# A limit on outstanding bytes beside a limit on outstanding transfers

## The chip, the cores and the metric

The kernel runs on one core of a Trainium2 chip. The metric is the time of one execution on the device in microseconds (us), the median of the runs shown. The engines are TensorE (PE, with its weight loads PEld), VectorE (DVE), ScalarE (ACT), GpSimd (POOL) and SyncE (SP). Here SP does nothing but issue transfers between the chip's main memory and the on-chip buffers; ACT issues four of them, at the start.

## The reference

The inputs are q, k and v of 8 batches, 8 heads, 576 positions and 64 values. Two attentions are added, one over means of 4 neighbouring positions, one over a band of 7 positions. Their sum goes through a gated layer:

```python
q_d = q.reshape(B, H, Sd, factor, D).mean(axis=3)      # k_d, v_d likewise, factor 4
out_up = np.repeat(sm_attn(q_d, k_d, v_d), factor, axis=2)
mask = np.abs(pos[:, None] - pos[None, :]) < factor
out_local = softmax(where(mask, scale * q @ k.T, -1e9)) @ v
x = (out_up + out_local).transpose(0, 2, 1, 3).reshape(B, S, H * D)
h = gelu(x @ w_in)                                      # 512 -> 1024
u, v = h[..., :512], h[..., 512:]
v_n = (v - mean(v)) / sqrt(var(v) + 1e-6) * g_ln
gated = u * (einsum('ts,bsd->btd', w_sg, v_n) + b_sg[None, :, None])
out = x + gated @ w_out
```

w_in, w_sg, b_sg, g_ln and w_out are the same for all batches. w_in and w_out arrive as 64-bit numbers.

## The kernel before

The work is cut into some 2,100 small tasks with names. A long string, ORDER, gives their order by hand; each task's instructions are appended to the queues of its engines in that order, and every engine works its own queue off in order. Attention runs per pair of heads: 32 groups, 4 for each batch. After a batch's four groups its gated layer runs, and its PE work is laced between the attention groups of the next batches.

Names of a group's tasks (a number behind the letters is the group):

- `lq`, `lk`, `lv`, `lw` load q, k, the values for the pooled attention (v) and for the band (vw). q and k are 293 KB, vw 320 KB; v is two transfers of 224 KB, for the first four groups four of 96 KB.
- `S` is the band's scores on PE, `Y` the pooled scores (from group 4 on both together, `YS`). `mx`, `nx` are maxima and biases, `ea`, `eb`, `ec` the exponentials on ACT, `np`, `nq` the divisions. `T`, `U`, `t` transpose on PE, `pa` to `pe` copy the results out, `D` multiplies by the values (L604 for the pooled ones, L620 for the band's). `xa` to `xl` make the sum x and split it into a high and a low half.

In the gated layer `v` is the second half of x @ w_in (L722), `u` the first half, `s` the product with w_sg, `o` the product with w_out (all three are L800), and `os` stores 288 KB of the result.

The weights are loaded as 64-bit words, 512 KB at a time: `wy0` to `wy3` (the v half of w_in), `wz0` to `wz3` (the u half), `wr0` to `wr3` (w_out). Each goes through a chain of small tasks: `wu` (ACT, L346) and `wq` (ACT L334, or DVE L336) work on the two words, `wb` on DVE (L340, L342) shifts, `wt` (POOL, L350) adds, `wh` and `wl` make a high and a low half. `wq0` to `wq4` without a letter load w_sg.

`S0` and `S3` are preceded by 28 and 20 matmuls on zeros (L955), which take the place of the scores' psum buffer.

Every transfer goes through the function `dma` (L219 to L225). It issues on SP, or on ACT where the order says `/A` (`lk0`, `lq0`, `lq1`, `lw1`), and makes the new transfer wait until the one six places back in the program's order has landed. The wait stands in the issuing engine's queue; what is behind it on that engine stands too.

The order at the start, in which the loads stand between compute tasks:

```python
lk0/A ks0/P wy0 wqy0/V lk1/S ks1/P wby0 lq0/A wy3 S0 mx0 nx0/V lq1/A wuy0 wqy3/V wy2 wty0 wy1 why0/V wby3 lw1/A qs1/P
ea0 lq3 wuy3 qs0/P wly0/P wqy2/A S1 eb0 Y1 mx1 wby2 ...
```

Of the kernel before, what the change touches and what calls it, by code (L numbers as in the profile page):

```python
# [1 line left out]

# [189 lines left out]
gl7.2/V ua7.6 ua7.7 ok1 os6.3 ok0 os5.3 sa7.7 sm7.7/V sm7.6/P gh7.3/A gl7.3/P o7.4 oa7.4 o7.0 o7.5 oa7.5 o7.6 oa7.6  # L192
os7.3.0 os7.2 ok2 o7.2 oa6.3 oa7.2 os6.1 ok3 oa7.0 o7.1 oa7.1 o7.3 oa7.3 os7.1 o7.7 oa7.7 os7.0 os7.3.1
"""
DEPTH = 6
EARLY_S, EARLY_D = 4, 4
WARM = {"S0": 28, "S3": 20}
SIZES = {"ps": 8, "X": 10, "R": 38}
# [6 lines left out]
def kernel(  # L205
# [14 lines left out]
    DQ = {"S": nc.sync, "A": nc.scalar}  # L220
    moves = []

    def dma(e, **kw):
        move = DQ[e].dma_start(**kw)
        if len(moves) >= DEPTH:  # L225
            tc.add_manual_dep(move.ins, moves[-DEPTH].ins.name, mybir.DependencyInfo(mybir.DependencyClass.Sync, mybir.DependencyReason.DATA))
        moves.append(move)

    ENG = {"V": nc.vector, "A": nc.scalar, "P": nc.gpsimd}

# [74 lines left out]


    add("small", {"S": 0.5}, lambda e: dma("S", out=g_sb, in_=small), mb=0.01)
    add("b", {"S": 0.5}, lambda e: dma("S", out=b_sb, in_=b_sg.broadcast_to([P, S])), mb=0.3)


# [4 lines left out]
    def weight64(t, src):  # L315
# [12 lines left out]
        def load(e):  # L328
            weights[t] = buffers.tile(shape, F32, name=f"weight_{t}")
            dma("S", out=flat().bitcast(I32), in_=src)  # L330
# [684 lines left out]
```

## Time and profile before

| | |
|---|---|
| median of 3 runs | 578.76 us (578.58 to 580.44) |
| span of the profiled execution, first to last instruction | 578.3 us |
| median less that span | 0.5 us |
| mean granted TensorE clock | 0.991 |
| moved by transfers | 62.73 MB, mean 108 GB/s |

The page gives no other time for the profiled execution than its span; the three timed runs lie 0.3 to 2.1 us above it. Terms of a sum are therefore made against 578.3 us and then carried to the median.

In the profile a line such as `start length engine line out<-in xcount` gives times from the span's start; `L224` is the line of the transfer's issue, `SPq` and `ACTq` are issues by SP and ACT. "issue" in place of a releaser means that the profile shows nothing that the engine waited for. The queues of kind "instruction" load the engines' own instructions; they use the same transfer engines as the data.

### The profile page before, as it was taken

To read this page: it belongs to the slowest core of one execution; us is meant where nothing else is said; L and a number is where in the kernel's file an instruction comes from. 1 tells how busy PE (TensorE), PEld (TensorE's weight loads), DVE (VectorE), ACT (ScalarE), POOL (GpSimd) and SP (SyncE) were. 2 spreads that over 40 slices of the span, in tenths; PEclk is the share of its full clock that TensorE was granted. 3 is DMA by queue.
4 is the path that set the end of the run, shared out by engine and by line. 5 is a ranking of instruction groups with operands and counts; after the bars stand their busy time and mean duration, and the time that the engine had idled before them with its cause. 6 is when DMAs were issued, how large, how long until landed. Compare 5 with 4: busy or idle time off the path is not lost.

```text
span 578.3 us, 17588 instructions
## 1 busy us (share of the span) xinstructions
PE 562.3 (97%) x7040; PEld 524.0 (91%) x7040; DVE 420.8 (73%) x943; ACT 355.8 (62%) x1239; POOL 309.6 (54%) x391
## 2 busy tenths in 40 slices
PE   7986999999999999999999999999999999999997
PEld 5775899989998899979999899988999889998997
DVE  7987989878877886677567678878757687553552
ACT  4895996978775794475648596465825678211310
POOL 6685647776875546524567824375266743401330
PEclk9897999999999999999999999999999999999999
DMA  8879214263435031610216413143326330001102
GB/s 310 276 234 313 98 45 120 96 192 87 140 96 164 24 107 54 208 63 1 86 56 197 114 67 98 41 151 98 87 83 195 103 107 2 18 23 41 43 1 102
DMA packets 30609, 62.73 MB, mean 108 GB/s; under 512 B 3648, under 2 KB 3904, under 8 KB 30528
## 3 DMA queue, kind: packets, MB, share of 16 engines
q1 hardware_dynamic: 29952, 60.39, 33.1%
q8 instruction: 55, 0.90, 0.7%
q10 hardware_dynamic: 576, 1.23, 0.6%
q14 instruction: 26, 0.21, 0.1%
HBM read 52.17 MB, written 9.44 MB: 107 GB/s over the span
## 4 chain that ended last, share of the span: by engine, by line
PE 91%; DVE 4%; DMA 2%; ACT 2%; issue 1%; ACTq 0%; DVEq 0%
PE ps L800 55%; PE ps L722 18%; PE ps L604 4%; PE ps L620 3%; PE ps L455 3%; PE ps L543 3%; PE ps L476 3%; PE ps L552 2%; DMA R<-in_qT_dram 1%; PE ps L955 1%; ACT L523 1%; ACT pd L523 1%; DVE stats L485 0%; PE ps L448 0%; DMA R<-in_v_dram 0%
## 5 line engine op out<-in xcount | busy, mean ns | idle before, releaser
L800 PE MATMUL ps<-wsg_h,R 128*128 128x288 f32 x576 | 120.5, 296 | 0.0
L800 PE MATMUL ps<-X,weight_z 128*128 128x288 f32 x512 | 109.4, 297 | 0.0
L800 PE MATMUL ps<-R,weight_r 128*128 128x288 f32 x768 | 108.4, 297 | 1.0 <-ACT R L734 0.8
L800 PEld LDWEIGHTS ps<-R,weight_r 128*128 128x128 f32 x768 | 103.1, 188 | 2.2 <-ACT R L734 0.9
L722 PE MATMUL ps<-weight_y,X 128*128 128x512 f32 x320 | 99.1, 404 | 0.0
L515 ACT ACTIVATE X<-X,nb 128x64 f32<-128x64 f32 x280 | 93.6, 339 | 2.8 <-DVE nb L494 2.3
L800 PEld LDWEIGHTS ps<-wsg_h,R 128*128 128x128 f32 x576 | 94.0, 188 | 0.2 <-DVE R L791 0.2
L800 PE MATMUL ps<-wsg_l,R 128*128 128x288 f32 x320 | 92.5, 295 | 0.0
L800 PEld LDWEIGHTS ps<-X,weight_z 128*128 128x128 f32 x512 | 84.3, 188 | 0.5
L800 PE MATMUL ps<-R,weight_z 128*128 128x288 f32 x256 | 75.5, 295 | 0.0
L722 PEld LDWEIGHTS ps<-weight_y,X 128*128 128x128 f32 x320 | 59.4, 191 | 12.5
L838 DVE SCALAR_TENSOR_TENSOR vs<-ps,g_sb,b_sb 128x288 f32<-128x288 f32 x64 | 32.7, 514 | 49.3 <-PE ps L800 43.9
L232 ACT CAST R<-R 128x512 fp32r<-128x512 f32 (+2 forms) x41 | 26.0, 645 | 62.4 <-DVE R L845 35.2
L800 PEld LDWEIGHTS ps<-wsg_l,R 128*128 128x128 f32 x320 | 60.3, 188 | 0.0
L763 POOL TENSOR_TENSOR rs<-rs,nhalf 128x1 f32<-128x1 f32 (+1 forms) x40 | 25.5, 641 | 64.9 <-DVE rs L754 60.9
L515 ACT ACTIVATION_READ_ACCUMULATOR X<-X,nb 128x1 f32 x280 | 53.5, 191 | 0.0
L722 PE MATMUL ps<-weight_y,R 128*128 128x512 f32 x128 | 51.2, 400 | 0.0
L439 POOL TENSOR_TENSOR pairs<-R 112x256 f32<-112x256 f32 x56 | 44.4, 793 | 9.2 <-DMA R<-in_v_dram 9.2
L845 POOL TENSOR_TENSOR R<-R,vs 128x288 f32<-128x288 f32 x27 | 23.7, 880 | 47.1 <-DVE vs L838 32.0
L800 PEld LDWEIGHTS ps<-R,weight_z 128*128 128x128 f32 x256 | 48.2, 188 | 0.2
L232 ACT COPY R<-ps 112x288 f32<-112x288 f32 (+4 forms) x77 | 30.1, 419 | 27.5 <-PE ps L543 20.0
L791 POOL TENSOR_TENSOR R<-R,R 128x512 fp32r<-128x512 f32 (+1 forms) x22 | 30.6, 1393 | 28.4 <-DVE R L232 6.4
(124 smaller groups left out, 1197.3 us busy)
## 6 DMA issues: line engine op xcount, KB each, us to landing
R<-in_v_dram SPq DMA_DIRECT2D x56, 224.0 KB, 3.8
X<-in_vw_dram SPq DMA_DIRECT2D x31, 320.0 KB, 4.2
R<-in_kT_dram SPq DMA_DIRECT2D x31, 293.0 KB, 4.3
out_dram<-R SPq DMA_DIRECT2D x31, 288.0 KB, 3.0
R<-in_qT_dram SPq DMA_DIRECT2D x30, 293.0 KB, 4.0
weight_y<-in_w_in_dram SPq DMA_DIRECT2D x4, 512.0 KB, 6.0
weight_z<-in_w_in_dram SPq DMA_DIRECT2D x4, 512.0 KB, 6.1
weight_r<-in_w_out_dram SPq DMA_DIRECT2D x4, 512.0 KB, 6.6
```

The lines of the kernel that those rows point to most:

```text
L232: (nc.scalar.copy if e == "A" else ENG[e].tensor_copy)(**kw)
L439: ENG[e].tensor_tensor(out=pairs, in0=v[:, 0:2], in1=v[:, 2:4], op=ALU.add)
L455: nc.tensor.matmul(out=sp[i][os, c * KB:(c + 1) * KB], lhsT=q[hs, t * QB:t * QB + KB], rhs=k[hs, t * QB:t * QB + KB], start=not early, sto ...
L476: nc.tensor.matmul(out=st["sdv"][n][os, cs], lhsT=qd2[par][hs, i * QC:i * QC + HD], rhs=st["kd"][hs, ks], start=True, stop=True)
L515: nc.scalar.activation(out=st["ms"][:, t, :], in_=src, func=AF.Exp, bias=st["nb"][:, t:t + 1], scale=scale, accum_out=sums[par][:, t:t + 1])
L604: nc.tensor.matmul(out=out, lhsT=lhsT, rhs=pdt[ks, probs, h * QC:(h + 1) * QC], start=first, stop=last)
L722: nc.tensor.matmul(out=acc, lhsT=r32(l), rhs=r32(weights[f"y{k}"][:, 0, w]), start=(i == 0 and ks[0] == 0), stop=(i == len(ops) - 1 and ks ...
L763: nc.gpsimd.tensor_tensor(out=rs[0:n], in0=rs[0:n], in1=nhalf[0:n], op=ALU.pow)
L791: ENG[e].tensor_tensor(out=r32(dst), in0=vact[s][0][0:n], in1=vh[0:n, 0:DM], op=ALU.subtract)
L800: nc.tensor.matmul(out=acc[:, 0:HALF], lhsT=r32(l), rhs=r32(r), start=(first and n == 0), stop=(last and n == len(ops) - 1))
L838: nc.vector.scalar_tensor_tensor(out=vsb[i], in0=at["ps", "m", b, "s", i][:, 0:HALF], scalar=g_sb[:, i // 2:i // 2 + 1], in1=b_sb[:, half( ...
L845: ENG[e].tensor_tensor(out=u[:, half(i)], in0=u[:, half(i)], in1=vsb[i], op=ALU.mult)
```

## The change

A second limit is added: a transfer is issued only when it and those outstanding before it are at most 1,200 KB together. `dma` walks back over the transfers ahead, adds up their sizes, and puts the wait on the first one with which the sum would be over the limit, or on the one six places back, whichever comes first. As before it is one wait for each transfer, fixed when the program is built.

```diff
-DEPTH = 6
+DEPTH, FLYING = 6, 1200 * 1024
...
     def dma(e, **kw):
-        move = DQ[e].dma_start(**kw)
-        if len(moves) >= DEPTH:
-            tc.add_manual_dep(move.ins, moves[-DEPTH].ins.name, mybir.DependencyInfo(mybir.DependencyClass.Sync, mybir.DependencyReason.DATA))
-        moves.append(move)
+        move, size = DQ[e].dma_start(**kw), 4 * math.prod(kw["out"].shape)
+        ahead, flying = 0, size
+        while ahead < len(moves) and ahead < DEPTH and flying <= FLYING:
+            ahead += 1
+            flying += moves[-ahead][1]
+        if flying > FLYING or ahead == DEPTH:
+            tc.add_manual_dep(move.ins, moves[-ahead][0].ins.name, mybir.DependencyInfo(mybir.DependencyClass.Sync, mybir.DependencyReason.DATA))
+        moves.append((move, size))
```

No engine's instructions change their order; the waits do. `DMAHW0` to `DMAHW7` are the eight semaphores that transfers signal when they land; each new transfer takes one of them.

First place: the head of ACT's queue. R_149 is k and R_166 q of group 0, R_226 is q of group 1, X_241 vw of group 1, weight_y_154, 168 and 230 are wy0, wy3 and wy2; the L515 rows are the exponentials of group 0. Before:

```order
L224 DMA R_149<-in_kT_dram 128x586
L224 DMA R_166<-in_qT_dram 128x586
L224 DMA R_226<-in_qT_dram 128x586
L346 ACT_TABLE_LOAD
L346 ACTIVATE weight_y_154<-weight_y_154 128x512 [waits DMAHW1_49]
L224 DMA X_241<-in_vw_dram 128x640 [waits DMAHW3_49]
L515 ACTIVATE X_246,sums_86<-ps_199,nb_95 128x64 [waits DVE_49,PE_49]
L515 ACTIVATE X_246,sums_86<-ps_199,nb_95 128x64 x3
L346 ACTIVATE weight_y_168<-weight_y_168 128x512 [waits DMAHW5_49]
L334 ACTIVATE weight_y_230<-weight_y_230 128x512 [waits DMAHW6_49]
```

Now:

```order
L225 DMA R_149<-in_kT_dram 128x586
L225 DMA R_166<-in_qT_dram 128x586 [waits DMAHW0_49]
L225 DMA R_226<-in_qT_dram 128x586 [waits DMAHW2_49]
L351 ACT_TABLE_LOAD
L351 ACTIVATE weight_y_154<-weight_y_154 128x512 [waits DMAHW1_49]
L225 DMA X_241<-in_vw_dram 128x640 [waits DMAHW6_49]
L520 ACTIVATE X_246,sums_86<-ps_199,nb_95 128x64 [waits DVE_49,PE_49]
L520 ACTIVATE X_246,sums_86<-ps_199,nb_95 128x64 x3
L351 ACTIVATE weight_y_168<-weight_y_168 128x512 [waits DMAHW4_49]
L339 ACTIVATE weight_y_230<-weight_y_230 128x512
```

Both loads of q now wait (for k of group 0, and for k of group 1), and X_241 waits for weight_y_230 (DMAHW6), where it waited for k of group 1.

Second place: SP's queue around the first three weights r (wr0, wr1, wr3). R_998 is k of group 6. Before:

```order
L224 DMA X_938<-in_vw_dram 128x640 [waits DMAHW3_49,PE_49,Pool_49]
L224 DMA R_998<-in_kT_dram 128x586 [waits DMAHW4_49]
L224 DMA weight_r_1004<-in_w_out_dram 128x2x512 [waits DMAHW5_49]
L224 DMA weight_r_1006<-in_w_out_dram 128x2x512 [waits DMAHW6_49]
L224 DMA weight_r_1066<-in_w_out_dram 128x2x512 [waits DMAHW7_49]
L224 DMA R_1082<-in_v_dram 112x512 [waits DVE_49,DMAHW0_49,PE_49,Activation_49]
```

Now:

```order
L225 DMA X_938<-in_vw_dram 128x640 [waits DMAHW3_49,PE_49,Pool_49]
L225 DMA R_998<-in_kT_dram 128x586 [waits DMAHW4_49]
L225 DMA weight_r_1004<-in_w_out_dram 128x2x512 [waits DMAHW0_49]
L225 DMA weight_r_1006<-in_w_out_dram 128x2x512 [waits DMAHW2_49]
L225 DMA weight_r_1066<-in_w_out_dram 128x2x512 [waits DMAHW5_49,DMAHW3_49]
L225 DMA R_1082<-in_v_dram 112x512 [waits DMAHW4_49,DVE_49,DMAHW6_49,PE_49,Activation_49]
```

The three weights and the load behind them wait for nearer transfers than the sixth ahead of them.

More of the change, by code (lines that the diff above doesn't have):

```diff
@@ L1 @@
+import math
 from contextlib import ExitStack
```

## The prediction

> **What bounds the kernel now.** First the page: busy shares, the clock row, the transfer row and the queue that loads instructions.
>
> ```profile
> PE 562.3 (97%) x7040; PEld 524.0 (91%) x7040; DVE 420.8 (73%) x943; ACT 355.8 (62%) x1239; POOL 309.6 (54%) x391
> PEclk9897999999999999999999999999999999999999
> DMA  8879214263435031610216413143326330001102
> q8 instruction: 55, 0.90, 0.7%
> ```
>
> PE sets the end, and the transfer engines are full only in the first four slices, up to about 60 us. So I cut the span where PE stops or its clock drops. In the table of windows each row gives length, busy time (with instructions begun) of PE, PEld, DVE, ACT, POOL, then clock, transfer share and GB/s.
>
> ```profile
> 14.76:45.56 30.80, 28.50 (x700) 23.42 (x700) 27.98 (x65) 28.75 (x148) 23.04 (x25) 0.94 0.82 258
> 45.56:50.06 4.50, 0.01 (x2) 0.00 (x1) 1.85 (x4) 4.48 (x12) 2.93 (x2) 0.87 1.05 303
> 50.06:57.00 6.94, 6.94 (x33) 5.48 (x33) 6.26 (x11) 0.68 (x2) 4.19 (x5) 0.59 1.02 316
> 57.00:105.46 48.46, 48.46 (x601) 45.85 (x600) 44.92 (x88) 42.23 (x121) 30.75 (x32) 1.00 0.35 111
> 105.46:105.85 0.39, 0.00 (x1) 0.00 (x0) 0.39 (x2) 0.39 (x4) 0.39 (x1) 1.00 0.19 72
> 105.85:240.00 134.15, 134.15 (x1782) 126.64 (x1782) 103.31 (x237) 95.25 (x345) 83.91 (x107) 1.00 0.34 103
> ```
>
> From 50.06 to 240 us PE idles 0.4 us in all. Whatever the change does to PE's arrival in that stretch goes straight to the end, and only the first 60 us can be moved much. Two holes stand out there: 4.5 us without a matmul, then 7 us at a clock of 0.59. The list of waits and the chain of waits have no releaser for either stop of PE:
>
> ```profile
> PE ps L620 <- issue: 4.5, 1, 4.5
> PE ps L455 <- issue: 0.4, 1, 0.4
> 45.90:105.70 59.80, 55.40 (x632) 51.33 (x632) 52.93 (x102) 47.28 (x133) 38.12 (x39) 0.94 0.47 148
> ```
>
> Both stops fall inside a run of equal instructions. The instruction queue made 55 fetches of 0.90 MB for 14,080 PE and PEld instructions: 256 each. Between the two stops (third row) PE began 632 + 632 = 1,264 recorded instructions, 16 short of five such blocks; waiting instructions are not in those counts. So I read both stops as PE running out of instructions at a block's edge. The queue listing of two windows, 42 to 47.2 us and 47 to 48 us, agrees: in the first no instruction packet ran, in the second one did.
>
> ```profile
> q1 hardware_dynamic: 888, 1.71, 97.0%
> q8 instruction: 1, 0.02, 7.5%
> ```
>
> The fetch was kept off full transfer engines. What filled them is in the list of issues from 38.8 to 41 us (KB each, us from issue to landing):
>
> ```profile
> weight_r<-in_w_out_dram SPq DMA_DIRECT2D x3, 512.0 KB, 7.1
> R<-in_kT_dram SPq DMA_DIRECT2D x1, 293.0 KB, 4.7
> ```
>
> That is 3 x 512 + 293 = 1,829 KB (1.87 MB) under the rule of six. At the 328 GB/s of the 42 to 47.2 us window (1.71 MB in 5.2 us) they need 5.7 us.
>
> **The change, part by part.** Nothing is moved in any engine's queue; only waits of transfers are added, on SP and on ACT.
>
> *Start: a cost.* 293 + 512 + 293 KB may go at once (1,098). Then lq0 waits for lk0, wy3 for wy0, lq1 for lk1, wy2 for wy3 (293 + 512 + 512 = 1,317), and lw1, which ACT issues, for wy2 (320 + 512 + 512 = 1,344). Behind lw1 in ACT's queue stand the exponentials of S0, the table of weights y3 and the scaling of y2, and DVE's work on y2 waits for the last. ACT before (start, length), then DVE's y2 step:
>
> ```profile
> 1.17 0.93 ACTq L224 DMA_DIRECT2D R<-in_qT_dram  x2
> 6.11 0.70 ACT L346 ACTIVATE weight_y<-weight_y 128x512 int32<-128x512 uint32 x1 [2.68 <-DMA weight_y<-in_w_in_dram]
> 7.50 0.34 ACTq L224 DMA_DIRECT2D X<-in_vw_dram  x1
> 10.22 0.32 ACT L515 ACTIVATE X<-ps,nb 128x64 f32<-128x64 f32 x1 [3.42 <-DVE nb L494]
> 11.99 0.69 ACT L334 ACTIVATE weight_y<-weight_y 128x512 f32<-128x512 f32 x1
> 13.30 0.68 DVE L340 TENSOR_SCALAR ps<-weight_y 128x512 int32<-128x512 int32 x1
> ```
>
> wy0 lands at 6.1 us. After it, two 512 KB transfers now go one after the other. For each I take 3.8 us, between a lone 293 KB transfer (issued at 89.3 us) and a 512 KB one issued within 2.1 us of 613 KB of others (window 21 to 23.5 us):
>
> ```profile
> R<-in_kT_dram SPq DMA_DIRECT2D x1, 293.0 KB, 2.9
> weight_z<-in_w_in_dram SPq DMA_DIRECT2D x1, 512.0 KB, 4.4
> X<-in_vw_dram SPq DMA_DIRECT2D x1, 320.0 KB, 3.4
> R<-in_qT_dram SPq DMA_DIRECT2D x1, 293.0 KB, 3.1
> ```
>
> wy2 then lands at 6.1 + 7.6 = 13.7 (11.9 to 14.9). ACT issues lw1 (0.4 us with waking), and from the first exponential to the end of y2's scaling it takes 12.68 - 10.22 = 2.46 us: 16.6 us. DVE's step, at 13.30 before, moves by 3.3 us (1.5 to 4.5). PE's twenty warming matmuls and S3 wait for the end of that DVE work (chain of waits: start, length):
>
> ```profile
> 1.17 6.82 DMA R<-in_qT_dram
> 14.76 4.02 PE ps L955 x20
> 45.56 4.49 issue
> ```
>
> From there to 45.56 us PE is busy 28.50 of 30.80 us, so the slip is not made up: **+3.3 us** when PE reaches the block's edge. S0 itself slips too: lq0, issued at 1.17 and landed at 7.99, is now issued after lk0's landing and lands near 10; that is shorter and hidden under ACT's wait. Later loads slip by about as much as their users: the transfers' rate of the start falls from 325 GB/s to an estimated 279 (1,200 KB per 4.4 us).
>
> ```profile
> 5.00:24.00 19.00, 16.12 (x246) 11.38 (x245) 15.57 (x34) 12.93 (x63) 14.06 (x17) 0.91 0.89 325
> ```
>
> *The fetch: a gain.* At the edge, wr0 waits for older loads, wr1 for lk6 and wr3 for wr0. Ahead of the fetch stand at most 1,200 KB, more likely lk6 and wr0, 805 KB, for 1,829 before. At 328 GB/s that is 2.0 to 3.2 us less; the ends are 0 (the fetch does not care) and 4.5 (the stop goes). I take **-2.8 us**; 1.7 us of the stop remains.
>
> [...]
>
> *The clock: a gain.* After the empty 4.5 us PE works at half clock:
>
> ```profile
> 50.74 2.86 PE ps L722 x6
> 57.77 7.22 PE ps L722 x31
> ```
>
> 0.48 us each against 0.23. Of 6.94 us at 0.59, about 2.5 us is lost. The other dip of the clock row (slice 2) follows a stretch in which PE worked 3.02 of 5 us, on small matmuls:
>
> ```profile
> 10.00:15.00 5.00, 3.02 (x76) 2.27 (x75) 4.93 (x11) 4.78 (x25) 4.76 (x7) 0.98 0.99 375
> ```
>
> With 1.7 us of stop, matmuls on both sides, I take the clock to hold: **-2.5 us**; the other end is 0.
>
> *What then limits.* DVE is busy 6.26 of 6.94 us after the stop and feeds D4 (two steps of DVE that wait, the copy of probabilities, and D4's first matmuls):
>
> ```profile
> 57.80 0.28 DVE L232 COPY R<-ps 128x116 f32<-128x116 f32 x1 [0.29 <-PE ps L552]
> 58.57 0.69 DVE L340 TENSOR_SCALAR ps<-weight_r 128x512 int32<-128x512 int32 x1 [0.49 <-ACT weight_r L334]
> 62.99 0.29 DVE L232 COPY R<-ps 112x192 f32<-112x192 f32 x1
> 64.99 0.56 PE ps L604 x15
> ```
>
> That copy ends 1.7 us ahead of D4. DVE resumes 3.3 - 2.8 = 0.5 us late and can make up the 0.29 + 0.49 us that it waits for PE and ACT: it allows D4 some 2.0 us earlier, as PE's own sum does. The 0.39 us stop at 105.46 may shrink (-0.2); DVE's 44.92 of 48.46 us there may take as much back. Later bursts land up to 1 us later, under loads that are issued a group of heads ahead; I cost them at 0, and up to +0.5 if POOL's sums of v lose that cover.
>
> Sum: 3.3 - 2.8 - 2.5 = **-2.0 us** on the profiled 578.3. The median, 578.76, lies 0.5 us above that span and moves with it: **576.8 us**.
>
> **Rivals.**
>
> (a) *The stop stays.* The fetch gets its turn whatever is outstanding, or its delay has another cause; then only the start's slip is left: 578.76 + 3.3 = 582.1, slower. It decides at a stop of over 2.9 us with the low clock (3.3 - 1.6 = 1.7). For it: the fetch share is tiny. Against: no packet for 5.2 us while the transfer engines were 97% taken. [...]
>
> (b) *The stop shrinks, the clock drops all the same.* PE then gains 2.8 and loses 3.3: 579.3, no measurable change. For it: slice 2, where half-empty work was enough.
>
> (c) *The stop goes altogether*, and the start slips by 2.5 only: 2.5 - 4.5 - 2.5 = -4.5, cut to about -4 by DVE: 574.8.
>
> (d) *Data become late.* In the second full stretch (39 to 62 us) 7.06 MB now move at 279 instead of 307 GB/s, some 2.3 us later, and ACT's work on weights stands in order behind them: +2 on top of the forecast's terms at their poor ends, 581. Against: PE's first L800 work begins at 68.29 us and reads weights z, which were issued before 39 us.
>
> ```profile
> DMA packets 3502, 7.06 MB, mean 307 GB/s; under 512 B 348, under 2 KB 348, under 8 KB 3497
> 68.29 7.94 PE ps L800 x60
> ```
>
> (e) *The limit hardly binds*: 578.8. Against: the start's sums above.
>
> **How the numbers follow.** Forecast 0.40, (a) 0.18, (b) 0.22, (c) 0.10, (d) 0.06, (e) 0.04. The forecast's own range is 575.2 to 578.2. Leaving out most of (a)'s far end and the last of (c): 574.5 to 582.0. Under 0.3% (1.7 us) a change cannot be told from none. Faster: 0.35 of the forecast's 0.40 and all of (c), 0.45. Same: the forecast's rest, most of (b) and (e), 0.29. Slower: (a), (d) and a little of (b), 0.26.
>
> **What would show it.** In the changed profile: the first exponentials on ACT begin near 14 us, not 10.2; PE's warming matmuls near 18; PE's "issue" stop after D3's first half is 1 to 2.5 us; the clock row has no dip in slice 4; D4 begins near 63. A stop of 4 us or more, or a start that slips over 5 us, makes the forecast wrong; so does PE waiting for a load after 60 us.

## The result, and the profile after

The change makes the kernel slower by a little: a median of 582.50 us over 5 runs (581.66 to 585.15) against 579.39 us over 5 runs (578.58 to 580.47) of the kernel before. The ratio is 1.0058, with a 95% interval of 1.0034 to 1.0083. The profiled spans are 582.5 and 578.3 us. The profiled execution after took 584.33 us, 1.8 us over the median of its five runs, and had the lowest granted clock of the five (0.988, against 0.993 to 0.997). In the runs for which both figures are on record the time lies 1.75 to 2.12 us above the span, so the profiled execution before, whose time is not given, took some 580 us (an estimate). What is read from the two profiles below holds for these two executions; the medians differ by 3.1 us.

The page of the kernel after (PE's share, granted clock, share of the transfer engines):

```profile
PE 564.5 (97%) x7040; PEld 525.8 (90%) x7040; DVE 421.7 (72%) x943; ACT 356.3 (61%) x1239; POOL 310.9 (53%) x391
PEclk8979999999999999999999999999999999999999
DMA  6777821561434222520216323053226330001102
```

The clock row read 7 in slice 4 and reads 9 there now; a 7 has come in slice 3, and the 8 stands in slice 1 instead of slice 2. The transfer engines are no longer full in the first four slices (8, 8, 7, 9 before; 6, 7, 7, 7 now), and the slices behind carry what was left over.

PE's timeline of the kernel after (start, length, engine, line, out<-in, count, idle time before it and its releaser). All lines of the changed kernel are 5 higher than before from there on: L455 is L460, L604 is L609, L620 is L625, L955 is L960.

```profile
17.89 2.34 PE L960 MATMUL ps<-zeros 128*128 128x256 bf16 x20 [1.45 <-DVE R L347]
23.50 0.93 PE L460 MATMUL ps<-R,R 64*64 64x64 f32 x40 [1.03 <-DMA R<-in_kT_dram]
30.73 1.55 PE L609 MATMUL ps<-R,R 48*64 48x144 f32 x36 [0.82 <-DMA R<-in_v_dram]
47.01 0.81 PE L625 MATMUL ps<-R,X 64*64 64x58 f32 x40 [0.43 <-DMA X<-in_vw_dram]
54.89 0.45 PE L625 MATMUL ps<-R,X 64*64 64x58 f32 x14 [1.86 <-issue]
```

The start slips as forecast: the warming matmuls begin at 17.89 instead of 14.76 us. Then there are three waits for loads that were not there before, 2.28 us together. The stop of 4.49 us has become one of 1.86 us.

The same is seen in the table of windows (length, busy time of PE, PEld, DVE, ACT and POOL, clock, transfer share, GB/s). First after, from the warming to the stop, the stop, and 5 to 24 us:

```profile
17.89:53.02 35.13, 30.61 (x700) 25.40 (x700) 28.54 (x65) 29.92 (x151) 22.59 (x24) 0.90 0.78 230
53.02:54.89 1.87, 0.01 (x2) 0.00 (x1) 1.83 (x4) 1.87 (x6) 1.21 (x1) 1.00 0.74 253
5.00:24.00 19.00, 12.29 (x184) 8.31 (x183) 13.67 (x27) 11.94 (x57) 11.41 (x14) 0.91 0.74 234
```

The stretch from the warming to the stop holds the same 700 + 700 instructions as before and took 30.80 us there, with PE busy for 28.50. It now takes 4.33 us more: 2.22 us of more idle time, which is about what the three waits for loads add up to, and 2.11 us of more busy time. Most of the latter is the clock. Half of it was granted after in three windows, and before in two. Of the stretch up to the stop they cover 6.83 us after and 3.41 us before, with PE busy all the time; half of the difference, 1.7 us, is my estimate of the time that this costs, from the matmuls of L722 in the profile before: 6 in 2.86 us at half clock (0.48 us each), 31 in 7.22 us at the full one (0.23). The rows of the windows, first after, then before:

```profile
10.97:14.38 3.41, 3.41 (x40) 2.04 (x32) 2.71 (x6) 0.41 (x3) 2.41 (x5) 0.50 0.78 249
31.45:38.28 6.83, 6.83 (x149) 6.39 (x140) 4.61 (x11) 5.54 (x31) 3.62 (x4) 0.50 0.67 195
55.34:58.76 3.42, 3.42 (x9) 2.64 (x10) 3.39 (x7) 2.21 (x6) 1.28 (x2) 0.50 0.78 273
```

```profile
14.78:18.20 3.42, 3.42 (x17) 2.36 (x17) 3.35 (x9) 3.39 (x18) 1.74 (x2) 0.50 1.01 354
48.92:55.74 6.82, 5.68 (x27) 4.49 (x27) 5.04 (x9) 1.80 (x4) 4.42 (x6) 0.50 1.02 312
```

From the start of the n-th instruction that PE and PEld recorded, in the traces of both kernels, the slip of after against before can be followed:

```text
n-th instruction of PE and PEld          before    after    slip
   300  warming before S3 runs            14.93    18.00   +3.07
   600  D of group 0                      25.99    31.05   +5.06
 1,697  last before the stop              45.35    52.81   +7.46
 1,700  after the stop                    50.06    54.89   +4.83
 1,760  half clock after the stop over    56.79    60.62   +3.83
 2,200                                    76.59    80.98   +4.40
 3,000  the stop at 105 us over          106.14   109.91   +3.77
14,000                                   569.33   573.61   +4.28
```

So the sum that came about is +3.1 (start) +4.3 (late loads and clock between the start and the stop) -2.6 (stop) -1.0 (clock after it) +0.5 (the rest) = +4.3 us of span. The forecast had +3.3, nothing, -2.8, -2.5, nothing. What failed is mostly the second term; the fourth, the clock behind the stop, came 1.5 us short.

### The profile page after: what moved, and what is told of

The parts are those of the page before. It is cut to its first block, busy times and chain, and to the rows that moved or that the text cites. A ratio compares the mean times of both kernels' runs of the same rounds, so it can differ in the third digit from the quotient of the medians.

```text
span 582.5 us, 17586 instructions
## 1 busy us (share of the span) xinstructions
PE 564.5 (97%) x7040; PEld 525.8 (90%) x7040; DVE 421.7 (72%) x943; ACT 356.3 (61%) x1239; POOL 310.9 (53%) x391
## 5 line engine op out<-in xcount | busy, mean ns | idle before, releaser
L850 POOL TENSOR_TENSOR R<-R,vs 128x288 f32<-128x288 f32 x27 | 23.7, 881 | 46.8 <-DVE vs L843 31.9
L237 ACT COPY R<-ps 112x288 f32<-112x288 f32 (+4 forms) x77 | 30.0, 417 | 21.3 <-PE ps L548 13.7
```

What stands on the lines that cost most here:

```text
L237: (nc.scalar.copy if e == "A" else ENG[e].tensor_copy)(**kw)
L850: ENG[e].tensor_tensor(out=u[:, half(i)], in0=u[:, half(i)], in1=vsb[i], op=ALU.mult)
```

## The experiments

In what follows "the limit" is the change's 1,200 KB. In most kernels it is confined to a part of the transfers, which are numbered in the program's order: the 44th is wr0. Unless an edit says otherwise it is made in the changed kernel.

### The limit from wr0 on, and the limit up to wr0

```diff
-        ahead, flying = 0, size
-        while ahead < len(moves) and ahead < DEPTH and flying <= FLYING:
+        ahead, flying, most = 0, size, FLYING if len(moves) >= 43 else 1 << 40
+        while ahead < len(moves) and ahead < DEPTH and flying <= most:
...
-        if flying > FLYING or ahead == DEPTH:
+        if flying > most or ahead == DEPTH:
```

The second kernel has `< 43` in place of `>= 43`. Expected of the first, and then of the second:

> The 1,200 KB limit holds only from the 44th transfer on (the first weights r); the start's loads go by the rule of six, as before. Theory A (the limit at the start makes loads late and costs PE 7.5 us by D3; at the weights r it shortens the stop of PE): PE reaches the stop at about 45.6 us, as before, the stop is 1 to 2 us, and the time is 2.5 to 5 us under the kernel before: 574 to 576.5. Rival B (the stop is shorter in the changed kernel only because PE comes later, when the weights have landed): the stop stays at 4 to 4.5 us, and the time is that of before within 1 us.

> The limit holds only for the first 43 transfers. Theory A: PE reaches the stop at 52 to 53.5 us, as in the changed kernel, and the stop is back at 4 to 4.5 us: 584 to 587 us. Rival B: the stop stays short, at about 2 us, and the time is that of the changed kernel, 582 to 583.

Measured: with the limit from wr0 on 575.29 us (573.84 to 578.96, 12 runs), ratio 0.9940 (0.9916 to 0.9964) to the kernel before; with the limit up to wr0 587.97 us in one run, where the median of before beside both was 579.33. Waits of PE and the clock row, first of the late limit:

```profile
PE ps L625 <- issue: 2.3, 1, 2.3
PEclk9999999999999999999999999999999999999999
```

```profile
PE ps L625 <- issue: 3.0, 1, 3.0
PE ps L460 <- DMA R<-in_qT_dram: 2.5, 1, 2.5
PE ps L460 <- issue: 1.3, 1, 1.3
```

With the late limit PE reaches the edge 0.6 us earlier than in the kernel before, not 7 us later, and the stop is 2.3 us all the same. So with PE on time the limit on the transfers around wr0 shortens the stop. But it is shorter with a late PE too: with the limit up to wr0 it is 3.0 us, between my 4 to 4.5 and the rival's 2 (the time is 1.0 us over my range). There PE is 9.5 us late at the edge, with a new stop of 1.3 us one block of 256 instructions earlier included. The whole change is about the sum of a loss at the start and a gain at wr0 (spans of +7.9 and -4.3 us, against +4.3 for both together), and the loss is the larger.

The stop is not the larger part of the late limit's gain. Its profiled execution has the full clock throughout (0.996 to 1.000 over its 12 runs; 0.990 to 1.000, median 0.993, in 16 runs of the kernel before beside it). The kernel before had PE busy for 9.1 us at half clock in the two rows shown above, which costs some 4.6 us (half of it, an estimate). Together with the 2.2 us of the stop that is more than the 4.3 us of span gained, so about 2.5 us were lost again in other waits.

### ACT's own transfers freed

Only SP's transfers are limited; those that ACT issues have the rule of six (`most` is `FLYING if e == "S" else 1 << 40`).

> The limit holds for SP's transfers; the four that ACT issues wait only by the rule of six, as before. Rival C (the slip comes from ACT's queue standing behind lw1): ACT's first exponentials are back near 10.2 us, PE reaches the stop near 46.5 us, and the time is about 576. Theory A (the slip after 18 us comes from loads that arrive at 235 instead of 325 GB/s): the first exponentials are early, but D0 still begins 4 to 5 us later than before, PE reaches the stop at 50 to 53 us, and the time is 580 to 582.

Measured: 584.42 us in one run. ACT's first exponential is back at its old time, and the slip is not gone. Timeline of ACT, DVE and PE:

```profile
10.20 0.32 ACT L520 ACTIVATE X<-ps,nb 128x64 f32<-128x64 f32 x1 [3.38 <-DVE nb L499]
15.72 0.69 DVE L345 TENSOR_SCALAR ps<-weight_y 128x512 int32<-128x512 int32 x1 [0.81 <-ACT weight_y L339]
17.19 4.14 PE L960 MATMUL ps<-zeros 128*128 128x256 bf16 x20 [1.63 <-DVE R L347]
48.33 1.34 PE L625 MATMUL ps<-R,X 64*64 64x58 f32 x40 [1.98 <-DMA X<-in_vw_dram]
```

DVE's step on y2 begins at 15.72 us, against 16.42 with the change and 13.30 before. It comes 0.7 us behind the landing of wy2 (15.00), and with the change 2.9 us behind it (13.48). So ACT's queue behind lw1 did cost over 2 us, but with ACT's loads beside it wy2 lands 1.5 us later, and the net gain is 0.7 of the 3.1 us. D0 is still 4.8 us late, and later a load of vw is waited for. The rival that blamed ACT's queue alone falls. My own range was missed as well: PE reaches the stop at 55.04 us, where I expected 50 to 53, and the time is 2.4 us over it. The half clock took much of that, as a table below shows.

### Eight warming matmuls fewer

```diff
-WARM = {"S0": 28, "S3": 20}
+WARM = {"S0": 20, "S3": 20}
```

This is the kernel before, with 16 instructions of PE and PEld less ahead of S0.

> The kernel before, with 20 in place of 28 warming matmuls ahead of S0: 16 PE instructions fewer; transfers as before. If PE stops because its instructions run out at the edge of a block of 256, it stops again after 1,697 recorded instructions, which is 8 matmuls further on in D3, for 3.5 to 4.5 us; time within 1 us of before. If it stops for something at that place of the program (data, a semaphore), it stops after 1,681.

Measured: 581.75 us in one run. Timeline of PE behind the stop, first of the kernel before and then of this one:

```profile
50.06 0.69 PE L620 MATMUL ps<-R,X 64*64 64x58 f32 x14 [4.49 <-issue]
```

```profile
51.20 0.33 PE L620 MATMUL ps<-R,X 64*64 64x58 f32 x6 [3.50 <-issue]
```

Of the same run of equal matmuls 14 stood behind the stop, and now 6: the stop has moved 8 matmuls on. Counted from the span's start it comes after the same number of instructions. The rows of the windows up to the stop, of before, of after and of this kernel:

```profile
0.00:45.56 45.56, 39.39 (x848) 31.21 (x849) 38.42 (x101) 35.27 (x172) 32.53 (x45) 0.96 0.83 276
```

```profile
0.00:53.02 53.02, 42.42 (x848) 33.71 (x849) 39.22 (x101) 35.78 (x173) 32.59 (x45) 0.90 0.74 226
```

```profile
0.00:47.70 47.70, 38.90 (x848) 31.16 (x849) 38.99 (x101) 35.73 (x173) 32.48 (x45) 0.96 0.84 274
```

848 + 849 = 1,697 each time. The place of the stop is set by the number of instructions, not by the work or its data. That fits a fetch of instructions in blocks (55 packets of the instruction queue for 14,080 instructions on the page of before, 256 each) better than a wait of a matmul for its data. The other kernels below agree. Their traces and the three of before, after and this kernel hold 21 waits of PE of over 0.25 us without a releaser, and each stands at this edge or a whole number of 256 instructions from it (one block before, 5 and 39 behind; instructions that only wait are counted too). The time is 2.4 us over the median of before beside it (579.33), where I had expected at most 1 us; it is one run, and those of before go from 575.41 to 581.69 us apart from one at 586.91.

### A smaller limit, on six transfers alone

`most` is `800 * 1024 if 43 <= len(moves) < 49 else 1 << 40`.

> The limit is put on six transfers alone, from wr0 (the 44th transfer) to X (the 49th), and is 800 KB there; every other transfer has only the rule of six. Theory A (the stop is a fetch of instructions held up by what is outstanding; the late limit gains until DVE becomes the bound): at the edge after 1,697 recorded PE instructions about 512 to 740 KB are outstanding instead of 1,024, so the stop falls from 2.30 us (limit of 1,200 KB from there on) to 0.5 to 1.5 us; but in the run with the late limit PE already waits 0.9 us for DVE at 64.5 us, and this wait grows by as much as the stop shrinks: 574.5 to 576.5 us, no better than 575.29. The stop at 105 us (0.39 us) comes back, since nothing limits the transfers there. Rival E (the stop has a fixed part, and what the limit took away was something else): the stop stays at 1.9 to 2.3 us.

Measured: 579.77 us (578.11 to 580.80, 10 runs), beside a median of before of 578.62, ratio 1.0005 (0.9990 to 1.0020). The profiled execution is the slowest of the ten. The stop is 1.1 us as expected, and nothing of the gain is left at the end. Waits of PE, of DVE between 48 and 66 us, and of ACT between 40 and 75 us:

```profile
PE ps L625 <- issue: 1.1, 1, 1.1
PE ps L609 <- DVE R L237: 2.2, 2, 1.4
```

```profile
DVE ps L345 <- ACT weight_r L339: 4.0, 1, 4.0
```

```profile
ACT weight_r L351 <- DMA weight_r<-in_w_out_dram: 5.4, 1, 5.4
```

With 800 KB only one quarter of wr can be on its way. The stop at 105 us is back with 0.5 us. wr1 and wr3 land at 51.2 and 54.6 us, where the limit of 1,200 KB from wr0 on had 48.3 and 50.2. ACT stands 5.4 us for them, DVE 4.0 us behind ACT, and PE behind DVE. At the 1,760th instruction PE was 5.8 us ahead of the kernel before, and at the 2,200th 0.2 us behind it; the half clock from 61.59 to 68.42 us, in which PE was busy for 5.5 us, took about 2.8 of these 6.0 us (half of the 5.5). My expectation had only a wait of DVE that grows by the length of the stop; it left out that the limit makes the weights late, and the clock.

### A limit of 1,600 KB

```diff
-DEPTH, FLYING = 6, 1200 * 1024
+DEPTH, FLYING = 6, 1600 * 1024
```

> The change with 1,600 KB in place of 1,200. Theory A (rate goes with what is outstanding; stop goes with what is outstanding): the start runs at 280 to 310 GB/s between 5 and 24 us instead of 234, the first exponentials slip by about 1 us instead of 3.8, the first D group by 1 to 2 us instead of 5; three quarters of wr (1,536 KB) may be out at the edge, so the stop is 3 to 4 us. 578.5 to 581 us. Rival F (the loss comes from waiting for a landing before an issue, at whatever limit): rate of 235 to 250 GB/s and the first D group 4 to 5 us later, about 583 us.

Measured: 583.36 us in one run, beside a median of before of 578.62. The window of 5 to 24 us:

```profile
5.00:24.00 19.00, 16.25 (x199) 10.83 (x197) 14.21 (x30) 13.23 (x61) 12.64 (x17) 0.82 0.81 263
```

The rate is 263 GB/s: 234 with 1,200 KB, 325 with the rule of six alone. It does go with the limit, as the first theory has it, but by less than I gave it (280 to 310). The first exponential is 2.2 us late instead of 3.8 and the first D group 3.6 us instead of 5.1; both lie between the two expectations, and the time is that of the rival. The stop is 2.4 us, shorter than the 3 to 4 that I gave. No size of this limit is shown to be harmless at the start.

### The limit on the transfers 9 to 43 alone

`most` is `FLYING if 8 <= len(moves) < 43 else 1 << 40`. The eight transfers of the start and all from wr0 on have the rule of six alone.

> The 1,200 KB limit only for the transfers 9 to 43 (from the transfer of X for V's first rows to the last one before wr0): the first eight, which feed the weight sums and the first S group, go as before. Theory A (the lower rate leaves later loads behind by more than their users slip): the first exponentials and the warming before the second S group start within 0.5 us of before (10.2 and 14.8 us), the rate from 13 to 30 us is near 235 GB/s, and the first D group starts 1.5 to 3.5 us later than before with a wait for a transfer of k or v ahead of it; the stop stays at 4 to 5 us; 580.5 to 583 us. Rival G (what I predicted: later loads slip by as much as their users, so without a slip at the start there is none): first D group within 0.5 us of before, 578.5 to 580 us.

Measured: 585.20 us in one run, 2.2 us over the end of what I expected, and 6.6 over the median of before. The window of 13 to 30 us, first before and then here, and PE's waits between 17 and 53 us:

```profile
13.00:30.00 17.00, 14.55 (x262) 11.01 (x260) 15.50 (x34) 15.38 (x83) 12.41 (x13) 0.90 0.88 294
```

```profile
13.00:30.00 17.00, 13.10 (x218) 10.05 (x221) 15.00 (x32) 15.31 (x82) 11.01 (x13) 0.91 0.81 231
```

```profile
PE ps L625 <- DMA X<-in_vw_dram: 1.6, 1, 1.6
PE ps L481 <- ACT R L237: 1.2, 1, 1.2
```

Here the warming begins only 0.4 us late, and the first D group 1.5 us late, without a wait for k or v ahead of it. The load of vw at 44 us is what PE then waits for, and at the edge PE is 6.8 us late, nearly as late as with the whole change (7.5). But most of that is the clock. The stretch from the warming to the stop, and two windows of half clock in it:

```profile
15.18:52.37 37.19, 33.25 (x700) 27.93 (x700) 29.15 (x66) 30.55 (x154) 22.62 (x24) 0.82 0.80 234
26.84:33.67 6.83, 6.73 (x116) 6.31 (x117) 5.43 (x14) 5.16 (x28) 3.35 (x5) 0.50 0.65 177
43.91:50.73 6.82, 6.39 (x126) 5.97 (x130) 3.67 (x10) 3.95 (x18) 3.20 (x5) 0.50 0.83 250
```

The same stretch in all twelve kernels, in us:

```text
                            length   PE idle   PE busy at half clock
before                       30.80     2.30        3.41
the change                   35.13     4.52        6.83
limit up to wr0              37.26     5.29        9.60
SP's transfers only          37.85     4.28       13.83
limit of 1,600 KB            34.26     4.47        4.22
transfers 9 to 43            37.19     3.94       13.12
the six without a limit
  on the early loads     30.2-32.9   2.3-4.2     0-3.4
```

PE's busy time less half of the last column is 26.7 to 27.7 us in every kernel, so what differs in busy time is mostly clock. In this kernel idle time makes 1.6 us of the loss in the stretch and the clock 4.9. So the later loads do not slip just as much as their users: without a slip at the start that is worth naming, PE stands for vw. The five kernels that limit the early loads also have more half clock there than the seven that do not. No run shows whether late loads bring these windows about. Where I missed: I put the loss at the first D group and expected a stop of 4 to 5 us. It was 1.4 us, with no limit on wr.

### Nine outstanding instead of six

```diff
-        if len(moves) >= DEPTH:
-            tc.add_manual_dep(move.ins, moves[-DEPTH].ins.name, ...
+        deep = 9 if 43 <= len(moves) < 56 else DEPTH
+        if len(moves) >= deep:
+            tc.add_manual_dep(move.ins, moves[-deep].ins.name, ...
```

This is the kernel before with a deeper rule for wr and what follows it.

> The kernel before with nine transfers allowed outstanding instead of six for the transfers 44 to 56 and nothing else: about 2,500 to 2,900 KB are outstanding at the edge after 1,697 recorded PE instructions, instead of 1,829 to 2,080. Theory A (the stop is a fetch that takes its turn behind outstanding bytes): the stop grows from 4.49 to 5.5 to 7.5 us, 580 to 583 us. Rival H (the stop depends only on the transfers that were ahead of the fetch when it was asked for some 300 instructions earlier, or on nothing of the kind): stop of 3.5 to 4.8 us, 578.5 to 580.5 us.

Measured: 579.32 us in one run; the stop is 4.7 us. Waits of PE, and the queues from 41.89 to 46.79 us:

```profile
PE ps L621 <- issue: 4.7, 1, 4.7
```

```profile
DMA packets 819, 1.57 MB, mean 321 GB/s; under 512 B 51, under 2 KB 51, under 8 KB 819
q1 hardware_dynamic: 819, 1.57, 99.1%
```

When the stop began, eight transfers of 2,661 KB together were outstanding, against 2,080 KB in the kernel before, and the stop is nearly the same (4.68 and 4.49 us). The first theory in its simple form, that the stop grows with what is outstanding at the stop, falls. All 819 packets of those 5 us are data; the instruction packet came right behind, at 46.8 us.

### What the fetch waits for

The records of the instruction queue allow a closer look. Of the 660 fetches in the twelve traces none begins more than 0.03 us before PE is 293 instructions (waiting ones counted too) ahead of the edge, and in every trace one begins within 0.16 us of that; I take this as the moment at which the fetch is asked for, which is an inference. From there to the fetch's packets, from those to PE's going on, and the stop, in us:

```text
                        outstanding   asked     packets'  end of packets   stop
                        when asked    to packets  time     to PE going on
before                   1,829 KB       5.00      1.20         1.59        4.49
nine outstanding         2,277          4.95      1.31         1.73        4.68
eight fewer to warm      1,984          3.78      1.16         1.74        3.50
limit up to wr0          1,733          6.43      1.29         1.62        2.96
transfers 9 to 43        2,373          3.50      0.88         1.68        1.44
limit of 1,600 KB        1,221          3.82      1.19         1.54        2.43
limit, wr0, wr1, wr3 only  805          3.63      1.32         1.50        2.98
limit from wr0 on        1,125          3.33      0.89         1.37        2.30
the change               1,125          2.70      1.00         1.45        1.86
SP's transfers only        805          2.17      0.90         1.46        1.22
limit for 44th to 90th   1,125          1.76      1.09         1.36        0.87
800 KB for six             613          2.30      0.88         1.51        1.06
```

PE goes on 1.4 to 1.7 us after the fetch's last packet in every row. So the stop is the sum of the three columns less the time for which PE still has work (3.2 to 3.6 us in nine of the rows, 4.1 to 6.4 in the three in which PE waits for something else meanwhile). The delay is 1.8 to 3.8 us with some 600 to 1,220 KB outstanding, and 3.5 to 6.4 with more. The two groups meet, and the amount alone does not give it: the three rows with 1,125 KB range from 1.8 to 3.3 us. What is issued between the asking and the packets goes with the delay in these rows: nothing at 1.76 us, one weight of 512 KB at 2.70 and at 3.33. With 805 KB it is 512 KB at 2.17 us and 1,248 KB at 3.63. But a longer delay also leaves more time for issues, so this does not show which brings the other.

### The limit where it helps

Two kernels follow from this: the limit for the 44th to the 90th transfer only (`43 <= len(moves) < 90`), and for the first three weights r only (`43 <= len(moves) < 46`: wr0, wr1 and wr3, the third of which the expectation calls wr2).

> The limit of 1,200 KB only for the transfers 44 to 90 (from wr0 to about 140 us); all others have the rule of six alone. The run with the limit from wr0 to the end lost 0.5 us against the kernel before between the PE instructions 8,850 and 8,900 (at about 330 us), where the limit held back a transfer of X. Theory A (the limit is worth something only where a fetch of instructions falls into a burst of transfers, and costs elsewhere): as the run with the late limit up to 300 us (stop of about 2.3 us at 45 us, none at 105 us), without the loss at 330 us: 574.3 to 576 us. Rival: nothing lost at 330 us comes from the limit, or the clock falls by chance as it does in some runs: 576 to 578 us.

> The limit of 1,200 KB only for the three transfers 44 to 46 (wr0, wr1, wr2); all others have the rule of six alone. Theory A, made sharper (the fetch that PE waits for at 45 us is asked for 293 instructions ahead, at about 42 us, and is late by what was issued ahead of it, so only wr0 to wr2 matter; with nine outstanding in place of six the stop was 4.68 us, no longer than the 4.49 us of before): stop of 2.0 to 2.6 us as with the limit on all later transfers; the stop of 0.39 us at 105 us is back; the second half of wr and the transfers of v behind it land as early as in that run or earlier: 574.5 to 577 us. Rival I (every transfer that is outstanding at the stop counts): v, X and the gate's weights are issued sooner and the stop is 3 to 4.5 us, 577 to 579.5 us.

Measured: 574.41 us for the first (573.78 to 574.95, 4 runs), ratio 0.9914 (0.9890 to 0.9938); 576.13 us for the second (574.16 to 578.25, 9 runs), ratio 0.9944 (0.9924 to 0.9964), both against 579.26. PE's waits between 40 and 110 us, first of the one, then of the other:

```profile
PE ps L625 <- issue: 0.9, 1, 0.9
PE ps L481 <- DVE R L632: 0.8, 1, 0.8
PE ps L805 <- DVE X L468: 0.3, 1, 0.3
```

```profile
PE ps L625 <- issue: 3.0, 1, 3.0
PE ps L460 <- issue: 0.8, 1, 0.8
```

The first has no stop at 105 us either; but neither have the kernels with the limit up to wr0 and with nine outstanding, which limit nothing there. Its profiled execution has the full clock from start to end (0.997 to 1.000 over the four runs). It loses nothing at 330 us, where the limit from wr0 on lost 0.4. That loss is not the limit's, though: the kernel with eight fewer warming matmuls, which has no limit, loses 0.4 us at the same place, and the one with 800 KB 0.6. The time is the fastest of all the kernels here and lies in the first range, near its lower end, with a stop of 0.9 us where I expected 2.3; its lead over the limit from wr0 on (0.9 us of the medians) is smaller than the intervals.

With the first three weights alone the time is the one I expected, but the stop is 3.0 us, over my 2.0 to 2.6 and at the edge of the rival's 3 to 4.5. The profiled execution is the slowest of the nine (578.25 us), so this stop need not be that of the others. wr1 and wr3 land at 49.7 and 51.4 us, 1.4 and 1.2 us later than with the limit from wr0 on, not as early as I expected. The transfers behind wr3 can have had little part in the stop: the first of them was issued at 45.55 us, 0.2 us before the fetch's packets. I read the 3.0 us as the same spread in which the three rows with 1,125 KB differ, whose cause stays open.

## Why the prediction was wrong

The forecast was 576.8 us, faster; it is 582.5, slower, above the range. One term that was put at nothing failed, and a second, the clock, did not come in.

**The start (+3.3): right.** wy2 lands at 13.48 us (13.7 forecast), ACT's first exponential begins at 13.97 (near 14), DVE's step on y2 at 16.42 (16.6), the warming matmuls at 17.89 (near 18). The slip is 3.1 us.

**"Later loads slip by about as much as their users": the step that failed.** It made the slip of the start the whole loss, and it rested on an estimated 279 GB/s. Two things were wrong in it. The rate is 234 GB/s in the window for which I had put 279: whole transfers do not fill 1,200 KB. At the issues between 5 and 24 us only 805 to 1,125 KB are outstanding, the new transfer included, and each takes 3.6 to 6.2 us to land, where I had put 4.4 us for 1,200 KB. And a lower rate is not a shift. The 19 us from 5 to 24 us move 234 instead of 325 GB/s, which is 1.7 MB less, and that many bytes are 7 us at the new rate, against a slip of 3 to 4 us in what uses them. The last of the four transfers of v for D0 lands at 31.2 us instead of 23.5. Before, it came 2.2 us ahead of D0's start at 25.68, and the loads of k and vw that PE now waits for came 2.3 and 1.8 us ahead of theirs. So PE waits for k, v and vw, 2.3 us in all. That is the half of the 4.3 us that the step is shown to have missed; 1.7 of the other half is half clock, whose cause stays open. The run with the limit on the transfers 9 to 43 shows the step's failure with hardly a slip at the start: 1.6 us of idle time more up to the stop, beside 4.9 us of half clock.

**The fetch (-2.8): right in kind, its size partly luck.** The stop went from 4.49 to 1.86 us, -2.6. The reading of "issue" as an instruction fetch at a block's edge is borne out by the run with eight warming matmuls fewer and by the 21 stops at whole blocks; that the limit on wr shortens it, by the run with the limit from wr0 on, -2.2. But kernels with the same 1,125 KB outstanding when the fetch is asked for stop for 0.87 to 2.30 us, and in two in which PE was late without a limit on wr the stop fell to 2.96 and 1.44 us. So how much of the 2.6 us is the limit's is not shown. My figure of why (bytes ahead of it, divided by the rate) is too simple, as the table of the fetch shows. At this one edge PE stopped in all twelve kernels, for 0.87 to 4.68 us. Between 41.89 and 46.79 us with nine outstanding, 819 data packets of the trace, a mean of some 51 for each of the 16 transfer engines against which the page counts all queues (819/16), went before the one of instructions. So the fetch got no early turn in the 5 us after the moment at which I take it to be asked for; when it reached the transfer engines, no trace shows.

**The clock (-2.5): a second term that failed.** What could be won was 2.8 us (half of the 5.68 us of busy time in the row of 48.92 to 55.74), near what I took. But of the pair of half-clock windows after the stop one came all the same (55.34 to 58.76), which leaves -1.0. Another pair came earlier, at 31.45, and ahead of the stop the clock costs 1.7 us more than before. Over the five runs the granted clock was 0.988 to 0.997, median 0.994; in the runs of the kernel before beside the experiments it was 0.990 to 1.000, with medians of 0.993 and 0.994. So the change gained nothing there. With the limit from wr0 on the gain did come (0.996 to 1.000). I had counted on the clock as if the length of the stop decided it. In the twelve traces a window began during the stop or within 1.7 us behind it after stops of 1.86, 2.43, 2.96, 2.98, 3.50, 4.49 and 4.68 us, and none after 0.87, 1.06, 1.22, 1.44 and 2.30 us. The length goes with it, but does not decide it by itself, and the windows ahead of the stop are another matter.

**What then limits.** DVE does allow PE more than the 2.0 us I gave it: with the limit from wr0 on PE is 5.4 us ahead after the stop, and still 4.2 us ahead after a wait of 0.9 us for DVE at 64.5 us. That term was never reached by the change.

**The rivals.** By its time the case is closest to (a), 582.1, but for none of (a)'s reasons: the stop did shrink. By its mechanism it is (d), data that become late, which I gave 6 in 100, joined to the clock of (b), which dropped all the same; I had looked for it in the second full stretch of transfers, from 39 us, where it came only with 800 KB, and not in the first. Of the signs named, "a start that slips over 5 us" did not appear, and no load is waited for after 60 us; D4 begins at 68.8 us instead of near 63. The sign that was missing from my list is PE's waits for loads between 18 and 50 us.

## What to carry to other kernels

A limit on outstanding bytes was paid for in rate here, where the transfer engines had been busy for 0.89 of the time (325 GB/s became 234 from 5 to 24 us). The lower rate was not a constant shift (the warming matmuls came 3.1 us late, the last load of v for D0 7.7 us): work out at every use how far the load lands ahead now, and how far behind the missing bytes put it. A stop of an engine without a releaser, in the middle of equal instructions, should be counted in instructions: if it comes at the same count in another variant, as here after 1,697 recorded instructions in three kernels, that points to the fetch of its code, and limiting the transfers around that moment can be worth it (the stop was 2.30 us instead of 4.49 with PE on time). Put such a limit only where the edge falls into a burst, and not so tight that the data behind it come late: here the limit there gave 0.9%, the limit everywhere cost 0.6%, and 800 KB in place of 1,200 gave nothing. Before a difference in time is put down to waits, compare PE's busy time and its granted clock; in one of these kernels the clock made 4.9 of 6.8 us.

## What the runs showed of the hardware that was not expected

- PE goes on only 1.4 to 1.7 us after the last packet of the instructions that it lacks, in all twelve traces of the table.
- With 1,200 KB allowed the transfers of the start moved 234 GB/s, with 1,600 KB 263, with six transfers (up to 2,442 KB) 325 GB/s. With 805 to 1,125 KB outstanding at the issues the transfer engines were busy for 0.74 of the time (5 to 24 us).
- All 21 waits of PE of over 0.25 us without a releaser in the twelve traces stand a whole number of 256 instructions apart, and of the 660 fetches in them none began more than 0.03 us before PE was 293 instructions ahead of the edge.
- In the rows shown the granted clock is 0.50 in windows of 3.41 to 3.42 us or 6.82 to 6.83, in stretches with PE wholly busy too (31.45 to 38.28 us after: busy 6.83 of 6.83 us). What triggers one stays open.
